# Chunked attention feeding a feed-forward layer on one core: a second buffer for transposed probabilities, moves halved over two queues, and attention groups placed elsewhere

## The chip, the cores and the metric

The kernel runs on one core of one Trainium2 chip. The metric is the device time of one execution in microseconds (us). Five engines work side by side: TensorE (PE, matrix products), VectorE (DVE), ScalarE (ACT), GpSimd (POOL) and SyncE (SP), which here only starts transfers; POOL starts transfers as well.

## The reference

```python
# q, k, v: [8 batches, 8 heads, 576 rows, 64]; chunks of 64 rows attend only to themselves
scores = scale * np.matmul(q_c, k_c.transpose(0, 1, 2, 4, 3))
scores = scores - np.max(scores, axis=-1, keepdims=True)
attn = np.exp(scores)
attn = attn / (np.sum(attn, axis=-1, keepdims=True) + 1e-09)
out = np.matmul(attn, v_c)
# x: [4608 tokens, 512], heads side by side; w_in 512 x 2048, w_out 2048 x 512
h = x @ w_in
g = np.where(h >= 1, h, np.where(h <= -1, 0.0, (h + 1) ** 2 / 4.0))
return (g @ w_out).astype(np.float32)
```

The weights come as float64.

## The kernel before

The 4608 tokens are worked in nine tiles of 512, t = 0 to 8. Tile 0 is the first 512 rows of batch 0 and tile 1 those of batch 1; tile 2 (SINGLE) is the last 64 rows of all batches; tiles 3 to 8 are the batches 2 to 7, taken in pairs (3,4), (5,6), (7,8).

**Weights.** Each of the 16 blocks of w_in (wi) and of w_out (wo) is loaded as 512 KB of words (`load_weight`, L258) and prepared on the chip (`prepare`, L275): ACT and DVE take the float64 words apart and write a high and a low part (parts_wi, parts_wo), with products in three terms afterwards. This is spread over tile 0: before the products of a block of the hidden layer, its weights must be ready.

**Feed-forward part.** For tiles 0 and 1 each of 16 steps j makes a hidden block (`ffn_in`, L560, PE into ps_h), the activation r, its rounding gh and remainder gl (`ffn_split`, L585: ACT L589, DVE L591), and two steps later the products with wo (`ffn_out`, L595) into four sums s = 0 to 3, in the banks ps_o0, ps_o1 and ps_o23, which holds both the third and the fourth. After j = 15 each sum is copied (`store`, L614: even ones by ACT L620, odd ones by DVE L618) into one of four buffers tmp and sent from there to DRAM by SP. Tile 2 (`single`, L936) and the pairs (`whole`, L987) use fewer products, of combined inputs and combined weights. The combined weights are made in tile 1 (`combine_weights`, L791), kept in the DRAM tensor combos, and come back through a ring of six half buffers, which POOL loads (L864). In a pair the second tile's hidden blocks go to DRAM (rest, `put_aside` L982) and come back into r (`fetch` L1017, POOL), and `second_half` (L1023) makes their outputs, during the next stage's products.

**Attention** runs in groups, four to a tile (two heads of a batch's 512 rows each, or the like). For a group: q and k are loaded (SP); `attn_turn` (L393) transposes them by DVE (L400, qT and kT); `scores_of` makes 64 x 64 products on PE into ps_a (L424); `attn_softmax` (L469) takes the maximum (DVE L480), subtracts it (DVE L496), the exponentials (ACT L499), sums (DVE L505), reciprocal (L506, L507) and product e <- e, sm (L512, by POOL for tile 0, else DVE), then a transpose into x (DVE L532) and eight transfers aT <- x (`move`, L518 to L524), of 32 partitions each. Finally `values_of` (L431, PE L446) multiplies aT with v. For tile 1 the subtraction and the sums are made by ACT: eight exponentials of 64 columns that add up as they go (L489). In tile 0 x is not used; PE transposes instead (L391).

The one buffer x is written by DVE and read by the eight moves of the group. Their queue is POOL for the tiles 1, 3 and 4, else SP. aT, v, q and k have two buffers each.

**Where the groups stand.** Tile 0's attention runs at the start; a table SECOND (L1094) puts the scores ("front") and values ("back") of tile 1's groups, and the front of tile 2's first group, at steps j of tile 0. In tile 1 every four steps a `burst` (L1120) takes the values of one group and the scores of the next: groups of tile 2, then the first of tile 3. In tile 2 bursts stand every 13 units of products from the 12th (tiles 3 and 4, with the scores of tile 5's first two groups in the last two), and in the pairs every 15 units.

**What sets the order.** The program does not write instructions engine by engine. Each part goes to a planner (`Plan`, L18 to L129) with an engine, a cost in us, what it reads and writes, and is written out in the order in which it would be ready by those costs; so an edit at one place can move instructions on all engines. Each engine, POOL's and SP's queues among them, works its own list in that order.

## Time and profile before

| | |
|---|---|
| Time, median of 3 runs | 861.07 us (858.66 to 862.81) |
| The profiled execution, its time | 861.77 us |
| Its span | 859.9 us |
| Mean clock granted to TensorE | 0.995 of full |
| PE busy | 830.0 us, 97% of the span |
| DVE busy | 559.2 us, 65% |
| ACT busy | 461.9 us, 54% |
| POOL busy | 276.2 us, 32% |
| Moved by the 16 DMA engines | 162.59 MB, mean 189 GB/s |

The span is the profiled part of the execution; its own time is 1.9 us longer. Idle time is named after what released the engine ("<- DVE h L908": the instruction that wrote h, at line 908). PE's busy time is counted from starts and modelled ends, so that a PE that is busy need not be at its best rate. By the trace's times, tile 0 ends at about 138 us, tile 1 at 228, tile 2 at 335, and the first pair's first half at 475.

### The profile page before, as it was taken

Reading aid. Unit: us, or ns where it says so; the run is one execution under the profiler, and the core shown is the slowest. Engines: PE = TensorE matmul, PEld = TensorE weight load, DVE = VectorE, ACT = ScalarE, POOL = GpSimd, SP = SyncE. Lnnn points to the kernel's source line nnn. Section 1 sums busy time; section 2 is a strip of 40 time slices with the busy share of each in tenths; the row PEclk is TensorE's granted clock in tenths of the full one; section 3 lists DMA queues with packets and bytes.
Section 4 is the critical chain, followed back from the end, with each engine's and each line's share of the span. In section 5 each row is a group of like instructions: output and inputs, shape, how many; then the busy total and the mean of one; then the engine's idle time right before and its main releaser. Section 6 shows DMA issues by size and latency. Waiting matters only on the chain.

```text
span 859.9 us, 16488 instructions
## 1 busy us (share of the span) xinstructions
PE 830.0 (97%) x5918; PEld 682.7 (79%) x5918; DVE 559.2 (65%) x991; ACT 461.9 (54%) x863; POOL 276.2 (32%) x498
## 2 busy tenths in 40 slices
PE   6998999999999997999999999999999999999998
PEld 6776777888887886888888788888887888888786
DVE  4899998999787875676579525665583234344322
ACT  4788884555455554555557324555582245455321
POOL 6235320253456551232232212332232123332210
PEclk9999999999999999999999999999999999999999
DMA  9989973676699996888778617865545254444432
GB/s 235 267 273 253 263 203 81 184 232 207 141 251 247 228 235 174 224 223 225 208 207 217 200 58 208 235 196 176 171 168 184 74 171 166 153 156 151 138 108 73
DMA packets 236368, 162.59 MB, mean 189 GB/s; under 512 B 190464, under 2 KB 203776, under 8 KB 236288
## 3 DMA queue, kind: packets, MB, share of 16 engines
q0 software_dynamic: 33664, 102.79, 36.3%
q1 hardware_dynamic: 201568, 58.50, 29.7%
q8 instruction: 47, 0.77, 0.4%
q10 hardware_dynamic: 1056, 0.26, 0.1%
q14 instruction: 33, 0.27, 0.1%
HBM read 116.39 MB, written 36.70 MB: 178 GB/s over the span
## 4 chain that ended last, share of the span: by engine, by line
PE 65%; issue 11%; DMA 8%; DVE 6%; POOL 6%; SPq 2%; ACT 1%; POOLq 0%; DVEq 0%; ACTq 0%
PE ps_o L604 34%; PE ps_h L885 20%; PE ps_h L570 8%; POOL ring L864 4%; DMA ring<-combos 2%; PE ps_a L446 2%; SPq L333 1%; DMA r<-rest 1%; PE ps_a L424 1%; DMA aT<-x 1%; DMA first_wi<-in_k_dram 1%; POOL rest L984 1%; DMA rest<-r 1%; DVE tmp L296 1%; DVE tmp L301 1%
## 5 line engine op out<-in xcount | busy, mean ns | idle before, releaser
L604 PE MATMUL ps_o<-parts_wo,gh 128*128 128x512 f32 x1152 | 360.5, 394 | 1.9 <-ACT gh L589 1.8
L604 PEld LDWEIGHTS ps_o<-parts_wo,gh 128*128 128x128 f32 x1152 | 212.0, 189 | 46.2 <-ACT gh L589 2.6
L604 PE MATMUL ps_o<-parts_wo,gl 128*128 128x512 f32 x576 | 225.5, 391 | 0.0
L864 POOL DMA_DIRECT2D ring<-combos x224 | 120.5, 539 | 238.7 <-PE ps_h L885 231.0
L591 DVE TENSOR_TENSOR gl<-r,gh 128x512 fp32r<-128x512 f32 x144 | 98.4, 686 | 103.5 <-ACT gh L589 102.9
L589 ACT CAST gh<-r 128x512 fp32r<-128x512 f32 x144 | 88.9, 620 | 137.7 <-PE ps_o L604 78.9
L604 PEld LDWEIGHTS ps_o<-parts_wo,gl 128*128 128x128 f32 x576 | 108.5, 188 | 24.1 <-DVE gl L591 1.4
L908 DVE TENSOR_TENSOR h<-ps_h,snaps 128x512 f32<-128x512 f32 (+1 forms) x96 | 58.9, 614 | 81.3 <-ACT snaps L699 72.9
L918 DVE SCALAR_TENSOR_TENSOR r<-h,r 128x512 f32<-128x512 f32 x88 | 60.2, 684 | 59.3 <-ACT r L917 59.1
L885 PE MATMUL ps_h<-t,ring 128*128 128x512 f32 x360 | 97.2, 389 | 0.0
L699 ACT COPY snaps<-ps_h 128x512 f32<-128x512 f32 (+1 forms) x96 | 50.9, 530 | 84.2 <-PE ps_h L885 83.4
L914 ACT ACTIVATE r<-h 128x512 f32<-128x512 f32 x88 | 55.6, 632 | 68.2 <-DVE h L908 66.5
L570 PE MATMUL ps_h<-xh,parts_wi 128*128 128x512 f32 x256 | 87.1, 398 | 0.8 <-DVE parts_wi L315 0.4
L885 PEld LDWEIGHTS ps_h<-t,ring 128*128 128x128 f32 x360 | 67.6, 188 | 14.0
L885 PE MATMUL ps_h<-xh,ring 128*128 128x512 f32 x192 | 74.9, 390 | 0.0
L917 ACT ACTIVATE r<-r 128x512 f32<-128x512 f32 x112 | 70.6, 630 | 2.6
L885 PE MATMUL ps_h<-b,ring 128*128 128x512 f32 x216 | 60.7, 390 | 0.0
L1020 POOL DMA_DIRECT2D r<-rest x48 | 25.7, 537 | 105.3 <-DVE gl L591 81.4
L885 PE MATMUL ps_h<-set,ring 128*128 128x256 f32 x336 | 50.4, 289 | 8.3 <-DVE h L908 5.5
L885 PEld LDWEIGHTS ps_h<-set,ring 128*128 128x128 f32 x336 | 46.0, 192 | 14.9 <-DVE h L908 6.0
L570 PEld LDWEIGHTS ps_h<-xh,parts_wi 128*128 128x128 f32 x256 | 48.0, 188 | 12.1 <-DVE parts_wi L315 0.9
L524 POOL DMA_DIRECT2D aT<-x x96 | 47.7, 501 | 28.4 <-issue 12.0
(166 smaller groups left out, 1127.3 us busy)
## 6 DMA issues: line engine op xcount, KB each, us to landing
ring<-combos POOLq DMA_DIRECT2D x224, 256.0 KB, 3.8
rest<-r POOLq DMA_DIRECT2D x48, 256.0 KB, 3.3
r<-rest POOLq DMA_DIRECT2D x48, 256.0 KB, 2.9
words_wi<-in_moe_w_in_dram SPq DMA_DIRECT2D x16, 512.0 KB, 7.5
words_wo<-in_moe_w_out_dram SPq DMA_DIRECT2D x16, 512.0 KB, 6.0
v_sb<-in_v_dram SPq DMA_DIRECT2D x128, 64.0 KB, 3.0
out_dram<-tmp SPq DMA_DIRECT2D x32, 256.0 KB, 3.8
combos<-x_parts POOLq DMA_DIRECT2D x32, 256.0 KB, 3.3
```

The costliest lines, as they stand in the source:

```text
L524: queues[queue].dma_start(out=aT[b:b + Q, to], in_=x[a:a + Q, of])
L570: nc.tensor.matmul(out=ps, lhsT=weight["wi", j][:, half, kc * P:(kc + 1) * P], rhs=x, start=(kc == 0 and i == 0), stop=(kc == KC - 1 and i ...
L589: plan.add("act", 0.52, lambda: nc.scalar.copy(out=gh, in_=now(r)), (rkey,), (ghkey,), ahead=ahead)
L591: plan.add("dve", 0.6, lambda: nc.vector.tensor_tensor(out=gl, in0=now(r), in1=gh.bitcast(F32), op=ALU.subtract), (rkey, ghkey), (glkey,), ...
L604: nc.tensor.matmul(out=acc, lhsT=x[:, cols], rhs=weight["wo", j][:, half, :], start=(j == 0 and i == 0), stop=(j == NF - 1 and i == 2),)
L699: "act", cost, lambda: nc.scalar.copy(out=out(), in_=src()), reads, writes, ahead=ahead
L864: plan.add("pool", 0.55, lambda: nc.gpsimd.dma_start(out=ap().bitcast(F32), in_=combos[d][:, n, :].bitcast(F32)), (f"dram{d}_{n}",), (key, ...
L885: nc.tensor.matmul(out=ps[:, :wide], lhsT=w()[:, at:at + P], rhs=y(), start=name in FRESH and i == 0 and k == 0, stop=i == 1 and k == 2, s ...
L908: plan.add("dve", 0.36 if wide == QC else 0.62, lambda: nc.vector.tensor_tensor(out=o(), in0=source[1](), in1=ap(), op=ALU.add), (source[0 ...
L914: plan.add("act", 0.52, lambda: nc.scalar.activation(out=now(r), in_=h(), func=AF.Relu, bias=0.5, scale=0.5), (hkey,), (rkey,), ahead=50)
L917: plan.add("act", 0.52, lambda: nc.scalar.square(out=now(r), in_=now(r)), (), (rkey,), ahead=50)
L918: plan.add("dve", 0.6, lambda: nc.vector.scalar_tensor_tensor(out=now(r), in0=h(), scalar=1.0, in1=now(r), op0=ALU.max, op1=ALU.min), (hke ...
```

## The change

1. **x and its moves.** From the tile 3 on, groups write x and the fourth tmp buffer in turn (x_pair). `move` takes one half: four transfers on SP and four on POOL, with a key each (aT's two halves); for tile 1 both halves stay on POOL.
2. **Stores** of the tiles from 1 on use only the first three tmp buffers.
3. **Sums by ACT** for tile 2's groups as well, as in tile 1.
4. **Places.** The front of tile 2's first group leaves tile 0; three backs (and the fronts beside them) come one step j later, or the last one. In tile 1 a table SPREAD sets the bursts. In tile 2 the last two bursts hold values only. The stage of pair (3,4) has ten bursts from its first unit on, every 13; that of (5,6) eight, every 15; that of (7,8) none.
5. **First loads.** The first three wi and two wo blocks go from SP's queue to POOL's, among the v loads.
6. **Smaller.** A transfer of combined weights to DRAM waits for a later weight to be prepared; the buffers into which `fetch` brings back the second half are taken in another order (r, two aside, r, instead of r, r, two aside).

```diff
+    x_pair = (x_bufs[0], tmp_bufs[3])
...
+    def spare(t):
+        return tmp_bufs[:3] if t > SINGLE - 2 else tmp_bufs
...
-        return emit, (akey, vkey), pkeys
+        return emit, (f"{akey}_0", f"{akey}_1", vkey), pkeys
...
-        sums = t == 1
+        sums = t in (1, SINGLE)
...
-        queue = "pool" if t in (1, SINGLE + 1, SINGLE + 2) else "sp"
...
+        def move(j, queue):
+
+            for i in range(4):
+                a, b = ((2 * j + n) * Q for n in divmod(i, 2))
...
-            xkey, x = x_bufs[turn(t, g) % len(x_bufs)]
+            xkey, x = x_bufs[turn(t, g) % len(x_bufs)] if t <= SINGLE else x_pair[turn(t, g) % 2]
...
-            plan.add(queue, 4.8, move, (xkey,), (akey,), lag=1.7, moving=0.4)
+            for j in range(2):
+                queue = "pool" if t == 1 or j else "sp"
+                plan.add(queue, 2.6, lambda j=j, queue=queue: move(j, queue), (xkey,),
+                         (f"{akey}_{j}",), lag=1.7 if t < SINGLE else 2.5, moving=0.4)
...
-        okey, o = turn_of("tmp", tmp_bufs)
+        okey, o = turn_of("tmp", spare(t))
...
-            plan.add("pool", 0.7, send, reads, (f"dram{d}_{n}",), lag=1.7, moving=0.8)
+            plan.add("pool", 0.7, send, (*reads, f"done_wo{max(2 * p + 1, 5)}"),
+                     (f"dram{d}_{n}",), lag=1.7, moving=0.8)
...
-        return (*r_bufs, aside(0), aside(1))[j % 4]
+        return (r_bufs[0], aside(0), aside(1), r_bufs[1])[j % 4]
...
-        ("q", 0, "sp"), ("k", 0, "act"), ("wi", 0, "sp"), ("q", 1, "sp"), ("k", 1, "sp"),
...
+        ("q", 0, "sp"), ("k", 0, "act"), ("wi", 0, "pool"), ("q", 1, "sp"), ("k", 1, "sp"),
...
-        1: ((front, 0),), 3: ((front, 1),), 5: ((back, 0), (front, 2)), 8: ((back, 1), (front, 3)),
-        11: ((back, 2),), 13: ((back, 3), (front, 4)),
+        1: ((front, 0),), 3: ((front, 1),), 6: ((back, 0), (front, 2)), 9: ((back, 1), (front, 3)),
+        12: ((back, 2),), 14: ((back, 3),),
...
+    SPREAD = {1: (None, 8), 4: (8, 9), 7: (9, 10), 10: (10, 11), 13: (11, 12), 15: (None, 13)}
...
-    run(units, range(12, 12 + 13 * 8, 13))
+    run(units, {12 + 13 * m: (12 + m, 14 + m if m < 6 else None) for m in range(8)})
...
-        run(units, range(8, len(units), 15))
+        n = turn(t, 0) + 2 * NP
+        if t == SINGLE + 1:
+            some = [(None, n), (None, n + 1)] + [(n + m, n + m + 2) for m in range(2 * NP)]
+            run(units, {13 * m: pair for m, pair in enumerate(some)})
+        elif n < ALL:
+            some = [(n + m, n + m + 2 if n + m + 2 < ALL else None) for m in range(2 * NP)]
+            run(units, {8 + 15 * m: pair for m, pair in enumerate(some)})
+        else:
+            run(units, {})
```

POOL's list at the start of the program, before (v_sb and first_wo hold v; e and first_wo the exponentials of tile 0):

```order
L366 DMA v_sb_72<-in_v_dram 64x4x64 x4
L366 DMA v_sb_73<-in_v_dram 64x4x64 x4
L366 DMA first_wo_148<-in_v_dram 64x4x64 x4
L366 DMA first_wo_146<-in_v_dram 64x4x64 x4
L512 TENSOR_TENSOR e_76<-e_76,sm_83 128x512
L837 DMA combos_101<-parts_wi_291 128x4x128 x2
L512 TENSOR_TENSOR e_77<-e_77,sm_84 128x512
L837 DMA combos_104<-parts_wi_380 128x4x128
L512 TENSOR_TENSOR first_wo_148<-first_wo_148,sm_83 128x512
L512 TENSOR_TENSOR first_wo_146<-first_wo_146,sm_84 128x512
```

and after the change (words_wi and words_wo are the weights' words):

```order
L268 DMA words_wi_175<-in_moe_w_in_dram 128x4x256
L268 DMA words_wi_179<-in_moe_w_in_dram 128x4x256
L370 DMA v_sb_72<-in_v_dram 64x4x64 x4
L275 DMA words_wo_200<-in_moe_w_out_dram 128x1024
L370 DMA v_sb_73<-in_v_dram 64x4x64 x4
L268 DMA words_wi_252<-in_moe_w_in_dram 128x4x256
L370 DMA first_wo_148<-in_v_dram 64x4x64 x4
L275 DMA words_wo_307<-in_moe_w_out_dram 128x1024
L370 DMA first_wo_146<-in_v_dram 64x4x64 x4
L516 TENSOR_TENSOR e_76<-e_76,sm_83 128x512
L516 TENSOR_TENSOR e_77<-e_77,sm_84 128x512
L516 TENSOR_TENSOR first_wo_148<-first_wo_148,sm_83 128x512
```

The weights' loads stand among those of v, and the four products of tile 0's softmax behind all of them (the fourth is the row after these); the first transfers of combined weights come later than these.

SP's list towards the end of tile 2, before (aT<-x x8 are the moves of the two groups of tile 5, out_dram the first store):

```order
L347 DMA k_sb_70<-in_k_dram 32x16x32 x4
L366 DMA v_sb_72<-in_v_dram 64x4x64 x4
L347 DMA q_sb_69<-in_q_dram 32x16x32 x4
L347 DMA k_sb_71<-in_k_dram 32x16x32 x4
L524 DMA aT_78<-x_80 32x256 x8
L366 DMA v_sb_73<-in_v_dram 64x4x64 x4
L347 DMA q_sb_68<-in_q_dram 32x16x32 x4
L524 DMA aT_79<-x_80 32x256 x8
L347 DMA k_sb_70<-in_k_dram 32x16x32 x4
L366 DMA v_sb_72<-in_v_dram 64x4x64 x4
L629 DMA out_dram<-tmp_136 64x512 x2
```

and after the change, with tmp_138 the second buffer for x:

```order
L370 DMA v_sb_73<-in_v_dram 64x4x64 x4
L525 DMA aT_78<-x_80 32x256 x4
L351 DMA q_sb_68<-in_q_dram 32x16x32 x4
L351 DMA k_sb_70<-in_k_dram 32x16x32 x4
L525 DMA aT_79<-tmp_138 32x256 x4
L370 DMA v_sb_72<-in_v_dram 64x4x64 x4
L370 DMA v_sb_73<-in_v_dram 64x4x64 x4
L351 DMA q_sb_69<-in_q_dram 32x16x32 x4
L351 DMA k_sb_71<-in_k_dram 32x16x32 x4
L525 DMA aT_78<-x_80 32x256 x4
L633 DMA out_dram<-tmp_136 64x512 x2
```

The moves on SP are four at a time instead of eight, and come from the two buffers in turn; the other four of each group stand on POOL's list.

PE's list where the second half of pair (5,6) starts, right after the last block of the sums before (parts_wo_507, in the change 502, is the first block of the new sums, j = 0, and 627 or 626 the second; ps_o_139 holds the third and the fourth sum), before:

```order
L604 MATMUL ps_o_141<-parts_wo_507,gh_131 128x512 x2
L604 MATMUL ps_o_141<-parts_wo_507,gl_133 128x512
L604 MATMUL ps_o_142<-parts_wo_507,gh_131 128x512 x2
L604 MATMUL ps_o_142<-parts_wo_507,gl_133 128x512
L604 MATMUL ps_o_139<-parts_wo_507,gh_131 128x512 x2
L604 MATMUL ps_o_139<-parts_wo_507,gl_133 128x512
L604 MATMUL ps_o_139<-parts_wo_507,gh_131 128x512 x2
L604 MATMUL ps_o_139<-parts_wo_507,gl_133 128x512
L885 MATMUL ps_h_143<-xh_1_92,ring_2134 128x512
L885 MATMUL ps_h_143<-xl_1_97,ring_2134 128x512
L885 MATMUL ps_h_143<-xh_1_92,ring_2134 128x512
L885 MATMUL ps_h_143<-t_3797,ring_2134 128x512 x3
```

and after the change:

```order
L608 MATMUL ps_o_141<-parts_wo_502,gh_131 128x512 x2
L608 MATMUL ps_o_141<-parts_wo_502,gl_133 128x512
L608 MATMUL ps_o_142<-parts_wo_502,gh_131 128x512 x2
L608 MATMUL ps_o_142<-parts_wo_502,gl_133 128x512
L608 MATMUL ps_o_139<-parts_wo_502,gh_131 128x512 x2
L608 MATMUL ps_o_139<-parts_wo_502,gl_133 128x512
L608 MATMUL ps_o_141<-parts_wo_626,gh_132 128x512 x2
L608 MATMUL ps_o_141<-parts_wo_626,gl_134 128x512
L608 MATMUL ps_o_142<-parts_wo_626,gh_132 128x512 x2
L608 MATMUL ps_o_142<-parts_wo_626,gl_134 128x512
L608 MATMUL ps_o_139<-parts_wo_502,gh_131 128x512 x2
L608 MATMUL ps_o_139<-parts_wo_502,gl_133 128x512
```

The fourth sum's products for j = 0 (the second pair of rows on ps_o_139 with parts_wo_502) have moved behind those of the first two sums for j = 1.

More of the change, by code (lines that the diff above doesn't have):

```diff
@@ L514, in attn_softmax @@
         ), (skey,), (ekey,), port=True)
-        queue = "pool" if t in (1, SINGLE + 1, SINGLE + 2) else "sp"
-        def move():
-            for j in range(2):
-                for i in range(4):
-                    a, b = ((2 * j + n) * Q for n in divmod(i, 2))
-                    to, of = (slice(h * HALF, (h + 1) * HALF) for h in divmod(i, 2))
-                    queues[queue].dma_start(out=aT[b:b + Q, to], in_=x[a:a + Q, of])
+        def move(j, queue):
+            for i in range(4):
+                a, b = ((2 * j + n) * Q for n in divmod(i, 2))
+                to, of = (slice(h * HALF, (h + 1) * HALF) for h in divmod(i, 2))
+                queues[queue].dma_start(out=aT[b:b + Q, to], in_=x[a:a + Q, of])
         if t == 0:
@@ L528, in attn_softmax @@
             plan.add("pe", 0.45, lambda: flip(ps, e), (ekey,), (pkey,), columns=T)
-            plan.add("act", 0.48, lambda: nc.scalar.copy(out=aT, in_=ps), (pkey,), (akey,))
+            plan.add("act", 0.48, lambda: nc.scalar.copy(out=aT, in_=ps), (pkey,), (f"{akey}_0", f"{akey}_1"))
         else:
-            xkey, x = x_bufs[turn(t, g) % len(x_bufs)]
+            xkey, x = x_bufs[turn(t, g) % len(x_bufs)] if t <= SINGLE else x_pair[turn(t, g) % 2]
             plan.add("dve", 0.6, lambda: nc.vector.transpose(
@@ L1118, in hand_over @@
             give("r2", ("r2_0", "r2_1"), F32)
+    SPREAD = {1: (None, 8), 4: (8, 9), 7: (9, 10), 10: (10, 11), 13: (11, 12), 15: (None, 13)}
     def burst(n, m):
-        some = []
-        if n is not None:
-            some.append(values_of(*AT[n]))
-        if m < ALL:
+        some = [values_of(*AT[n])] if n is not None else []
+        if m is not None:
             some.append(scores_of(*AT[m]))
         attn_products(*some, lag=0.8)
-        if m < ALL:
+        if m is not None:
             attn_softmax(*AT[m])
@@ L1130, in burst @@
             attn_split(*AT[n])
-        if m > 3 * NP and m + 1 < ALL:
+        if m is not None and m > 3 * NP and m + 1 < ALL:
             attn_turn(*AT[m + 1])
@@ L1134, in burst @@
             load_heads(*AT[n + 2], "v")
-        if m + 2 < ALL:
+        if m is not None and m + 2 < ALL:
             load_heads(*AT[m + 2], "qk")
@@ L1143 @@
             else:
-                n = 2 * NP + j // 4
-                if j % 4 == 0:
-                    attn_turn(*AT[n + 1])
-                    if j == 0:
-                        load_heads(*AT[n + 2], "qk")
-                if j % 4 == 2:
-                    burst(n, n + 1)
-                if j == NF - 2:
-                    attn_turn(*AT[3 * NP + 1])
-                if j == NF - 1:
-                    burst(None, 3 * NP + 1)
+                if j == 0:
+                    attn_turn(*AT[2 * NP])
+                if j in SPREAD:
+                    n, m = SPREAD[j]
+                    burst(n, m)
+                    if m + 1 < 3 * NP + 2:
+                        attn_turn(*AT[m + 1])
             ffn_in(t, j)
@@ L1172, with run @@
         push(1, j)
-    n = 3 * NP
-    def run(units, at):
-        nonlocal n
-        for k, unit in enumerate(units):
-            if k in at and n < ALL:
-                burst(n, n + 2)
-                n += 1
+    def run(units, bursts):
+        for n, unit in enumerate(units):
+            if n in bursts:
+                burst(*bursts[n])
             unit()
     units = [unit for p in range(NQ) for unit in single(SINGLE, p)]
-    run(units, range(12, 12 + 13 * 8, 13))
+    run(units, {12 + 13 * m: (12 + m, 14 + m if m < 6 else None) for m in range(8)})
     for slot, name in ((0, "t21"), (4, "t31"), (1, "t11"), (5, "b22"), (2, "t41")):
```

6 rows, old and new, of the table first_loads are left out of this document.

## Prediction

> **What bounds the kernel now.** I read the busy time by stage first, to see where TensorE (PE) stands idle and what is full there; then the waits of PE, longest first; then the timeline around the longest. The windows of 20 us hold, after the name of each engine, its busy us, then the clock granted to TensorE, the share of the DMA engines and GB/s:
>
> ```profile
> 0.00:20.00 20.00, 13.29 (x146) 12.12 (x146) 7.74 (x14) 8.37 (x14) 13.49 (x25) 1.00 1.04 225
> 20.00:40.00 20.00, 17.71 (x299) 14.40 (x300) 16.53 (x33) 15.18 (x28) 5.40 (x6) 1.00 0.95 278
> 40.00:60.00 20.00, 19.85 (x127) 16.45 (x126) 19.94 (x39) 17.02 (x50) 6.59 (x12) 1.00 0.87 245
> 60.00:80.00 20.00, 17.16 (x154) 13.38 (x153) 19.12 (x40) 17.29 (x51) 6.58 (x12) 0.91 1.01 283
> 120.00:140.00 20.00, 19.20 (x113) 15.02 (x112) 19.92 (x37) 12.22 (x22) 2.24 (x3) 1.00 0.45 107
> 280.00:300.00 20.00, 19.10 (x230) 16.73 (x229) 17.13 (x33) 10.53 (x22) 11.33 (x23) 1.00 0.92 228
> 320.00:340.00 20.00, 14.46 (x72) 11.88 (x71) 12.48 (x24) 9.44 (x19) 4.14 (x8) 0.91 0.71 181
> ```
>
> PE loses its time in two places. In the first tile VectorE (DVE) works 19 to 20 of each 20 us from 40 on, up to the last weights at about 130, so DVE sets the pace there; before 40 it stands idle for 11.4 us in all (7.9 and 3.5), while the DMA engines are full (1.04 and 0.95). In the third tile, up to 335, the DMA engines are again nearly full (0.92) and PE drops to 14.5 of 20 in the last window. What PE waited for:
>
> ```profile
> PE ps_h L885 <- DVE h L908: 5.5, 1, 5.5
> PE ps_a L446 <- ACT e L489: 4.3, 2, 2.6
> PE ps_h L885 <- DVE x L532: 1.4, 1, 1.4
> PE ps_h L885 <- DMA ring<-combos: 1.3, 2, 0.9
> PE ps_a L446 <- DMA aT<-x: 1.0, 1, 1.0
> ```
>
> The longest wait, 5.5 us, is in the third tile. Its timeline (start, duration, engine, line, and in brackets the idle time before and its releaser):
>
> ```profile
> 317.25 5.25 SPq L347 DMA_DIRECT2D k_sb<-in_k_dram  x4
> 322.61 5.04 SPq L524 DMA_DIRECT2D aT<-x  x8
> 327.74 2.75 SPq L366 DMA_DIRECT2D v_sb<-in_v_dram  x4
> 330.78 0.71 DVE L532 STREAM_TRANSPOSE x<-e 128x512 f32<-128x512 f32 x1 [6.71 <-DMA v_sb<-in_v_dram]
> 332.58 0.41 DVE L908 TENSOR_TENSOR h<-ps_h,snaps 128x256 f32<-128x256 f32 x1
> 333.04 1.65 PE L885 MATMUL ps_h<-set,ring 128*128 128x256 f32 x6 [5.54 <-DVE h L908]
> ```
>
> This is a chain through one buffer. The eight moves aT<-x of the head group before stand on SP's queue behind key loads and are issued from 322.61 to 327.65. Only when they have landed may DVE write x again; it stood 6.71 us for that (the bracket names the v load, which is issued last; the moves hold the buffer). DVE's next products, h at 332.58, come behind it, and PE behind those. The last window's clock, 0.91 over 20 us, is another 1.8 us lost; the same 0.91 stands in 60:80. Every other wait in PE's list is shorter than these.
>
> **Third tile: two x buffers, half moves on two queues.** Now consecutive groups write different buffers, so a move may be late by a whole burst before DVE stands. 5.5 and the clock's 1.8 go: 7.3. What is late next is the rest of that list: x 1.4, ring 1.3, aT 1.0, together 3.7. They come from the same traffic:
>
> ```profile
> 268.51 1.49 POOL L524 DMA_DIRECT2D aT<-x  x3
> 270.43 0.50 POOL L524 DMA_DIRECT2D aT<-x  x1 [0.43 <-DMA ring<-combos]
> 280.76 2.99 POOL L524 DMA_DIRECT2D aT<-x  x6
> L524 POOL DMA_DIRECT2D aT<-x x57 | 28.2, 499 | 14.4 <-DMA ring<-combos 7.2 <-DVE x L532 2.7 <-issue 2.1
> ```
>
> In this tile GpSimd (POOL) issues the moves between its ring loads (28.2 us for 57), and some wait for ring loads to land. With four on each queue POOL has half of that, and two groups' scores leave the tile, but SP takes four more: at 5.04 us for eight, 2.5 us more beside q, k and v. I take 1.9 of the 3.7, half, since halves land no earlier if the DMA engines stay full. Gain 9.2; bounds 3.6 (if full DMA engines add waits as long again as those three, 7.3 - 3.7) and 11.0.
>
> By the Trainium skill (TensorE: Matmul & The Clock Gate, Part 1: The HAM clock gate) the array's clock is halved only after an idle window of about 3.4 us. The trace agrees for the 5.5 us wait, and disagrees in 60:80, where 0.91 follows a wait of 2.59 (quoted next); by the rule the clock term of the first tile would be 0, by the row 1.8.
>
> **First tile without the third tile's group, weights on POOL's queue.** The rows of one group's work on DVE (mean ns before the last bar), and its exps on ScalarE (ACT):
>
> ```profile
> L400 DVE STREAM_TRANSPOSE qT<-q_sb 128x512 f32<-128x512 f32 x32 | 22.4, 701 | 0.0
> L480 DVE TENSOR_REDUCE mx<-ps_a 128x8 f32<-128x512 f32 x34 | 23.2, 684 | 2.6 <-PE ps_a L424 2.4 <-ACT xo L699 0.3
> L496 DVE TENSOR_TENSOR e<-ps_a,mx 128x512 f32<-128x512 f32 x29 | 19.8, 681 | 1.8 <-ACT tb L699 0.8 <-ACT ta L699 0.5 <-ACT xe L699 0.5
> L505 DVE TENSOR_REDUCE sm<-e 128x8 f32<-128x512 f32 x30 | 19.9, 664 | 5.9 <-ACT e L499 5.9
> L512 DVE TENSOR_TENSOR e<-e,sm 128x512 f32<-128x512 f32 x32 | 21.9, 684 | 0.1
> L532 DVE STREAM_TRANSPOSE x<-e 128x512 f32<-128x512 f32 x32 | 22.6, 707 | 11.6 <-DMA v_sb<-in_v_dram 6.7 <-DMA aT<-x 4.1 <-DVE gl L591 0.4
> L489 ACT ACTIVATE e<-ps_a,mx 128x64 f32<-128x64 f32 x32 | 9.5, 328 | 0.1
> L489 ACT ACTIVATION_READ_ACCUMULATOR e<-ps_a,mx 128x1 f32 x32 | 7.1, 221 | 0.0
> 76.82 1.34 PE L446 MATMUL ps_a<-aT,v_sb 64*64 64x64 f32 x32 [2.59 <-ACT e L489]
> ```
>
> Two transposes, maximum, subtraction, sum, product and x: 2 x 0.70 + 0.68 + 0.68 + 0.66 + 0.68 + 0.71 = 4.8 us leave the DVE-bound stretch. They go to the second tile, where sums by ACT save the subtraction and the sum of its four groups (0.68 + 0.66 each, 5.4 in all), so DVE has no more work there than now; ACT has 8 x (0.33 + 0.22) = 4.4 us by durations instead of one exp, but has slack in that tile (12.2 of 20 at 120:140), so that costs nothing; if that cover were gone, a wait like the 2.59 above, four times.
>
> The waits for exps (4.3 us by PE's list, the longer one the 2.59 above) need values that stand too close behind the next group's scores; in the new order one such place (the second back of the first tile) has as little work between as now, the other has more. DVE's pace hides most of that anyway: a term of PE there counts only where DVE is not later.
>
> The start:
>
> ```profile
> 16.33 3.46 SPq L333 DMA_DIRECT2D first_wi<-in_k_dram  x2
> 31.22 0.48 PE L570 MATMUL ps_h<-xh,parts_wi 128*128 128x512 f32 x1
> 32.63 1.04 POOL L512 TENSOR_TENSOR first_wo<-first_wo,sm 128x512 f32<-128x512 f32 x1 [2.20 <-DVE sm L507]
> ```
>
> The last key load now ends its issue at 19.8, behind three weight loads on SP; the last product by POOL runs at 32.63, and the first FFN product on PE at 31.22. With the weights on POOL, q and k stand alone on SP, and each queue gets its share of full DMA engines, so keys may come some 5 us earlier; but the same bytes must land before DVE can prepare weights, and all four products on POOL now stand behind all its 21 loads. DVE could fill at most its 11.4 us idle; I take 1.2 of it (near the lower end, 0, since the same bytes pass through engines at 1.04 and 0.95). Gain 4.8 + 1.2 = 6.0; bounds 1.6 (the longer exps wait stays, 2.6, with its clock, 1.8, and is not covered: 6.0 - 4.4) and 9.0 (DVE 4.8 and 4.2 of its idle time).
>
> **From the second tile to the third.** Stores have three buffers now, and the first x of the alternate buffer comes where the fourth of tmp is also used by the combination of weights: a DVE row must wait for half moves to land, with gl, x parts and store copies behind it. Nothing in the trace shows it; bounds 0 (the products behind it wait for PE anyway) and 2.5 (four moves by SP, half of 5.04). I take 0.8.
>
> **Stores in the pairs.** The fourth copy of a tile must wait until the first's transfer has landed; PE then waits to write that bank. Where the second tile of a pair starts:
>
> ```profile
> 646.12 0.58 ACT L620 COPY tmp<-ps_o 128x512 f32<-128x512 f32 x1
> 646.51 0.62 PE L604 MATMUL ps_o<-parts_wo,gh 128*128 128x512 f32 x2
> 646.73 3.02 SPq L625 DMA_DIRECT2D out_dram<-tmp  x4
> 647.19 0.62 PE L604 MATMUL ps_o<-parts_wo,gh 128*128 128x512 f32 x2
> out_dram<-tmp SPq DMA_DIRECT2D x4, 256.0 KB, 5.6
> 814.30 0.73 PE L604 MATMUL ps_o<-parts_wo,gh 128*128 128x512 f32 x2 [1.50 <-ACT gh L589]
> ```
>
> Three products take 0.68 (646.51 to 647.19). The new order puts 24 products between the end of the first sum and the next write of the last, so PE comes at 646.1 + 8 x 0.68 = 651.5. The copy is free at 646.73 + 5.6 + 0.69 for the copy = 653.0: a wait of 1.5. The like at 812 is about 1.4, but there PE already waits 1.50 for gh; it takes the place of that. At the first pair there is work for 32 products, no wait or 0.5. Net +1.0; bounds 0 and 5.6 (one full landing, more than all three waits).
>
> **Third pair's scores in the first pair's stage.** The stage from 335 to 475 has ten bursts instead of eight, and POOL now carries half moves between ring loads there too. PE loses nothing there now. Bounds -0.3 (SP relieved) and +16 (second rival); I take +0.5, near the rows of the third tile (ring 1.3 in all, under fuller DMA).
>
> **The sum.** The profiled execution's own time is 861.8 (0.7 above the median). 861.8 - 9.2 - 6.0 + 0.8 + 1.0 + 0.5 = 848.9, so 849.0 us. What a measurement of this kernel can tell from no change is about 0.5%, 4.3 us: 856.8 to 865.4 counts as the same.
>
> **Rivals.** First, the transfers and not the queues are the limit: at 1.04 and 0.95 in the first 40 us and 0.92 in 280:300 a load moved to another queue lands no earlier. For it: those rows. Against it: the 5.5 us chain hangs on one buffer, whatever the rate. Then the start gives 0, the first tile keeps the longer exps wait and its clock, half of them covered by DVE's pace (4.8 - 4.4 / 2 = 2.6), and the third tile gives the 7.3 alone: 861.8 - 7.3 - 2.6 + 2.3 = 854.2. This is also what the Trainium skill says (DMA: Bandwidth & Descriptors, Issuing engines are not separate DMA queues): starting transfers from several engines saves only the time to issue them.
>
> Second, slower: half moves delay the ring. In 18 bursts of the pairs' stages POOL issues four moves between ring loads. In the third tile ring waits were 1.3 us in all with eight moves a burst; if the whole products' ring, with no slack left, waited 1.3 in every burst, that is 18 x 1.3 = 23.4, and 849 - 0.5 + 23.4 = 872. It decides from 12.9 / 18 = 0.7 us per burst. Against it: the waits listed for PE name the ring for 1.3 us in all, so the ring has slack outside the third tile now, where POOL stands for the same loads without moves.
>
> Third, better: both exps waits and their clock go (4.3 + 1.8 = 6.1 by PE, if DVE has room) and DVE fills 4.2 of its idle start: first tile 9 or a little more, third tile 11.0, stores 0: 861.8 - 9.0 - 11.0 + 0.8 + 0.5 = 843.
>
> **How the numbers follow.** Forecast 0.53, first rival 0.20, third 0.13, second 0.08, and 0.06 for a sum of small waits that ends within 0.5%. The forecast's own range is 844 to 854; the range reaches to 841 below and to 858 above, for the first rival with 2 to 4 us of store waits. Faster 0.84 (0.53 + 0.20 + 0.13 less 0.02 of the first rival's upper end), same 0.08, slower 0.08.
>
> **What would show it.** Right: PE's wait for h of 5.5 is gone and DVE never stands over 2 us before x; no 0.91 near 320:340; the last weights of the first tile are ready at about 124 instead of 130; the second tile's first product comes 5 to 7 us earlier; waits of 1 to 2 us at ps_o, for ACT or DVE copies, at the pairs' middles. The first rival shows in an unmoved 31.2 and unmoved last weights; the second in waits for ring spread over 335 to 640. The forecast is wrong if PE's loss between 335 and 800 exceeds 5 us, or if the first tile ends less than 2 us earlier.

## The result and the profile after

The changed kernel takes 869.3 us (median of 10 runs, 866.5 to 874.2) where the kernel before takes 862.6 (10 runs beside it, 856.4 to 867.1): a ratio of 1.0095, 95% interval 1.0067 to 1.0123. It is slower by 6.7 us by the medians and by 8 by the ratio, where 12 us faster was forecast, and lies outside the range of 841 to 858. Each trace is of one execution (run 1's took 873.0 us, the longest of its six), and run 10's ratio leaves out one execution of 1661.8 us. The profiled execution took 867.3 us, its span is 865.5 and its mean clock 0.984 (before: 861.8, 859.9 and 0.995).

When each stage starts, by the first product of its kind in the trace, and how long it lasts (us):

| | before: start | length | changed: start | length | difference of lengths | forecast |
|---|---|---|---|---|---|---|
| start, until the first feed-forward product | 0 | 31.2 | 0 | 36.9 | +5.7 | with the next row |
| tile 0 | 31.2 | 103.8 | 36.9 | 99.0 | -4.8 | -6.0 in both |
| tile 1 | 135.0 | 93.2 | 135.9 | 94.0 | +0.8 | +0.8 with its end |
| tile 2 | 228.2 | 107.6 | 229.9 | 107.7 | +0.1 | -9.2 |
| pair (3,4), first tile | 335.8 | 133.1 | 337.6 | 134.0 | +0.9 | +0.5 |
| its second tile and (5,6) | 468.9 | 173.5 | 471.6 | 177.2 | +3.7 | +1.0 with the next row |
| the rest, to PE's last product | 642.4 | 213.3 | 648.8 | 211.8 | -1.5 | |

These add up to 4.9 of the 5.6 us by which the span grew. Tile 2 is as long as before although its wait of 5.5 us is gone, and tile 0 ends no earlier (135.9 against 135.0) although a whole group's work on DVE has left it. What PE waited for in the changed kernel (us in all, times, longest; a wait of 1.2 for kT and one of 0.3 are left out):

```profile
PE ps_a L450 <- DMA aT<-x: 5.2, 2, 3.5
PE ps_o L395 <- DMA first_wi<-in_k_dram: 4.7, 2, 3.3
PE ps_o L608 <- DVE tmp L622: 4.0, 2, 2.5
PE ps_o L395 <- DMA q_sb<-in_q_dram: 3.6, 2, 2.3
PE ps_a L450 <- DMA combos<-parts_wi: 2.4, 1, 2.4
PE ps_o L395 <- DMA k_sb<-in_k_dram: 1.7, 1, 1.7
PE ps_a L450 <- DMA aT<-tmp: 1.6, 1, 1.6
PE ps_h L890 <- DMA ring<-combos: 1.4, 1, 1.4
PE ps_h L1218 <- POOL ident masks.py:199: 1.4, 1, 1.4
```

The wait for h of 5.5 is gone, as forecast. In its place stand waits for moves (aT from x and from the second buffer, 5.2 + 1.6) and store copies (4.0). The two waits for exponentials, 4.3 in all, are now one of 2.4 that is named after combined weights (combos). The values that waited read only aT and v; at the same product (80 to 87 us) other kernels of the new order name the exponentials, so this is most likely the longer of the two. Windows that lost much, beside 80:100, which is shown in the last section (busy us of PE, PEld, DVE, ACT, POOL with instructions in brackets, then clock, DMA share, GB/s):

```profile
0.00:20.00 20.00, 12.14 (x116) 10.90 (x116) 7.01 (x12) 8.07 (x13) 13.32 (x26) 0.83 1.01 236
20.00:40.00 20.00, 16.48 (x236) 14.41 (x237) 12.45 (x27) 12.65 (x23) 5.16 (x6) 0.83 0.90 225
280.00:300.00 20.00, 18.44 (x226) 16.57 (x224) 17.48 (x34) 10.84 (x23) 7.71 (x15) 0.95 0.94 230
300.00:320.00 20.00, 16.50 (x113) 14.17 (x112) 9.63 (x18) 7.03 (x14) 7.96 (x16) 0.88 0.83 193
480.00:500.00 20.00, 17.46 (x150) 13.82 (x142) 16.73 (x31) 7.08 (x12) 4.70 (x9) 0.91 0.82 205
```

DVE is busy 7.01 + 12.45 us of the first 40, before 7.74 + 16.53: it stands idle 4.8 us longer. The clock is 0.95 and 0.88 in 280:320 (20 x 0.05 + 20 x 0.12 = 3.4 us), where before it was lowered once, for 1.8; it is 0.91 after 480 and 0.83 in the first 40 us, where it was 1.00.

**Tile 2.** The timeline of one group, from DVE's transpose on:

```profile
299.22 0.71 DVE L533 STREAM_TRANSPOSE x<-e 128x512 f32<-128x512 f32 x1
300.21 1.99 POOL L525 DMA_DIRECT2D aT<-x  x4
304.64 3.69 SPq L370 DMA_DIRECT2D v_sb<-in_v_dram  x4
308.42 2.47 SPq L525 DMA_DIRECT2D aT<-x  x4
314.55 1.03 PE L450 MATMUL ps_a<-aT,v_sb 64*64 64x64 f32 x32 [3.50 <-DMA aT<-x]
```

x is written at 299.9. POOL starts its half at 300.2. SP's half comes at 308.4, behind q, k and v loads, and lands after 314; the values wait 3.50 us for it. Half of a move is started 8 us late, and the values need both halves. The stage's own account closes: before 5.5 + 1.4 + 1.3 + 1.0 of waits and 1.8 of clock, 11.0; now 5.2 + 1.6 + 1.4 and 3.4, 11.6.

**Stores.** Where the first half of pair (3,4) ends:

```profile
478.77 1.54 SPq L629 DMA_DIRECT2D out_dram<-tmp  x3
483.72 0.69 DVE L622 COPY tmp<-ps_o 128x512 f32<-128x512 f32 x1 [2.17 <-DMA out_dram<-tmp]
484.47 0.73 PE L608 MATMUL ps_o<-parts_wo,gh 128*128 128x512 f32 x2 [2.54 <-DVE tmp L622]
```

The fourth copy (DVE, line 622) waits until the first store, issued at 478.77, has landed; PE stands 2.54 us for the bank.

**Start.** PE's longest wait there, 3.35 us until 26.64, is for the last key load. This is what transfers took from issue to landing in the first 26 us before:

```profile
k_sb<-in_k_dram SPq DMA_DIRECT2D x2, 128.0 KB, 7.2
first_wi<-in_k_dram SPq DMA_DIRECT2D x4, 128.0 KB, 7.9
```

and in the first 28 us of the changed kernel:

```profile
k_sb<-in_k_dram SPq DMA_DIRECT2D x2, 128.0 KB, 10.6
first_wi<-in_k_dram SPq DMA_DIRECT2D x4, 128.0 KB, 9.4
```

Keys land 10.6 and 9.4 us after their issue instead of 7.2 and 7.9. Taking the weights off SP's queue hardly let SP issue the keys earlier: the last pair starts at 15.52 instead of 16.33, the pair before at 10.09 instead of 9.96, because each issue took longer. With the weights' bytes now beside them, they land later. PE's waits before the first feed-forward product are 11.4 us (4.7 + 3.6 + 1.7 in the list above, and 1.4 for the identity matrix), before 8.9. Its work there takes longer too. The filling products, which only keep PE busy between loads, before and in the changed kernel:

```profile
L1213 PE MATMUL ps_h<-ident 128*128 128x128 f32 x56 | 9.1, 321 | 1.4 <-POOL ident masks.py:199 1.4
```

```profile
L1218 PE MATMUL ps_h<-ident 128*128 128x128 f32 x56 | 11.2, 373 | 1.4 <-POOL ident masks.py:199 1.4
```

At the clock of 0.83 of the first 40 us (before: 1.00) one of the 56 took 373 ns instead of 321. So 2.5 of the 5.7 us are waits and the rest is longer busy time (25.5 us against 22.4 up to that product), 2.1 of it in the filling products. The clock of 20:40 is 0.83 to 0.91 in all five kernels that load these weights on POOL's queue and 1.00 in all nine that load them on SP's; in 0:20 it is 0.74 to 0.84 in the five, and 0.91 in three of the nine.

### The profile page after: what moved, and what is told of

It is laid out like the page before. It is cut to its first block, busy times and chain, and to the rows that moved or that the text cites. A ratio compares the mean times of both kernels' runs of the same rounds, so it can differ in the third digit from the quotient of the medians.

```text
span 865.5 us, 16563 instructions
## 1 busy us (share of the span) xinstructions
PE 833.0 (96%) x5890; PEld 687.5 (79%) x5890; DVE 555.3 (64%) x987; ACT 468.7 (54%) x923; POOL 304.8 (35%) x551
## 4 chain that ended last, share of the span: by engine, by line
PE 81%; DMA 8%; DVE 5%; SPq 3%; issue 1%; POOL 1%; ACT 0%; DVEq 0%; POOLq 0%; ACTq 0%
PE ps_o L608 39%; PE ps_h L890 28%; PE ps_h L574 8%; PE ps_a L450 2%; SPq L337 2%; PE ps_a L428 2%; DMA out_dram<-tmp 1%; DMA first_wi<-in_k_dram 1%; DMA k_sb<-in_k_dram 1%; DMA aT<-x 1%; DMA words_wo<-in_moe_w_out_dram 1%; DMA combos<-parts_wi 1%; DMA q_sb<-in_q_dram 1%; SPq L525 1%; POOL combos L841 1%
```

## The experiments

Theory A is that each loss comes from what the change put on a queue or took from a buffer; B, that the DMA engines are full, whatever the queue; C, that the new places of the groups cost the time. In all diffs "-" is the kernel named and "..." stands for lines left out.

| run | us (median) | ratio to before, 95% interval |
|---|---|---|
| the change | 869.3 | 1.0095 (1.0067 to 1.0123) |
| 1 change, loads on SP | 869.2 | 1.0096 (1.0062 to 1.0130) |
| 2 change, moves of tiles 3, 4 on POOL | 863.6 | 1.0020 (0.9998 to 1.0042) |
| 3 change, one x, four store buffers | 860.2 | 1.0001 (0.9970 to 1.0032) |
| 4 change, these three undone | 855.2 | 0.9930 (0.9888 to 0.9972) |
| 5 before, loads on POOL | 863.6 | 1.0031 (0.9996 to 1.0067) |
| 6 before, three store buffers | 865.7 | 1.0048 (1.0018 to 1.0079) |
| 7 before, half moves on two queues | 859.8 | 0.9979 (0.9947 to 1.0011) |
| 8 as 4, tile 2's moves on POOL too | 848.4 | 0.9851 (0.9793 to 0.9908) |
| 9 change, SP's halves on ACT's queue | 876.2 | 1.0174 (1.0133 to 1.0215) |
| 10 before, tile 5's moves on POOL | 855.4 | 0.9927 (0.9901 to 0.9954) |
| 11 as 8, front of tile 2 back in tile 0 | 848.4 | 0.9863 (0.9827 to 0.9900) |
| 12 as 8, two x and three store buffers | 857.7 | 0.9969 (0.9941 to 0.9997) |

**1. The first loads back on SP.**

```diff
-        ("q", 0, "sp"), ("k", 0, "act"), ("wi", 0, "pool"), ("q", 1, "sp"), ("k", 1, "sp"),
+        ("q", 0, "sp"), ("k", 0, "act"), ("wi", 0, "sp"), ("q", 1, "sp"), ("k", 1, "sp"),
...
```

> The change with the list of first loads of before (weights on SP's queue again), all else as changed. Theory A (each loss is made by what the change put on a queue or took from a buffer): the weights on POOL's queue made the keys and the attention of the first tile late, so the first product of the feed-forward part comes back from 36.9 to about 31 us, VectorE's idle time before 40 us falls from 20.5 to about 16, and the first tile ends 4 to 5 us earlier than in the changed kernel: about 865 where the changed kernel has 869. Theory B (the transfers, not the queues, are full in the first 40 us): first product at 36 or 37, time within 1 us of the changed kernel. Theory C (the new places of the attention groups cost the time): the same as B.

The first feed-forward product came at 29.8 and tile 1 began at 131.3 instead of 135.9, as A said; the total did not move (869.2, where A had about 865). PE's waits:

```profile
PE ps_a L450 <- DMA aT<-x: 13.2, 3, 5.8
195.47 1.25 PE L450 MATMUL ps_a<-aT,v_sb 64*64 64x64 f32 x29 [5.84 <-DMA aT<-x]
```

The waits for moves grew from 5.2 to 13.2 us, one of 5.84 in tile 1 among them; there SP's half was started 2.0 us behind POOL's (188.4 against 186.4), after loads of q and k. So tile 1 begins 4.6 us earlier without these loads, and waits for half moves took it back. This trace is of an execution of 873.0 us; at the median of 869.2 the waits may be shorter. The step from "tile 0 ends earlier" to "the kernel ends earlier" failed.

**2. Moves of tiles 3 and 4 on POOL alone.**

```diff
-                queue = "pool" if t == 1 or j else "sp"
+                queue = "pool" if t in (1, SINGLE + 1, SINGLE + 2) or j else "sp"
```

> The change with both halves of the moves on POOL's queue for the groups of tiles 3 and 4 (as all eight were before); the two x buffers stay. Theory A: SP, which now starts 16 transfers a burst in tile 2's stage, is what makes half moves late, so PE's waits for aT (6.8 us in all in the changed kernel) and the lowered clock there (3.4 us) go, and ring waits of 1 to 2 us come: 5 to 9 us faster than the changed kernel, about 862. Theory B (the DMA engines are full there, 0.95): the waits move to the ring or stay, within 2 us of the changed kernel.

0.7% faster than the change, as A expected. No wait for aT is left in the list; those for store copies stayed (4.9 us), and waits for the ring came:

```profile
PE ps_h L890 <- DMA ring<-combos: 4.2, 5, 1.4
300.00:320.00 20.00, 20.00 (x207) 17.25 (x197) 14.37 (x27) 10.21 (x20) 13.28 (x27) 1.00 1.03 227
```

The clock in 300:320 is 1.00 again. Tile 2's stage takes 104.9 us instead of 107.7. This is A, with part of B: 2.8 of the gain came there, and the ring took 2.8 (4.2 - 1.4) of what the moves gave back.

**3. One x buffer and four store buffers.**

```diff
-    x_pair = (x_bufs[0], tmp_bufs[3])
+    x_pair = (x_bufs[0], x_bufs[0])
...
-        return tmp_bufs[:3] if t > SINGLE - 2 else tmp_bufs
+        return tmp_bufs
```

> The change with one x buffer for all groups and the four store buffers of before. Theory A: the waits for store buffers (4.0 us, with a lowered clock of 1.8 at 480:500) go; what the second x buffer saved is at most small here, since the moves are halves: 3 to 5 us faster than the changed kernel, about 865. The rival, that the second x buffer is worth its 5.5 us: VectorE's wait for x comes back with 4 to 6 us in tile 2's stage, and the time is that of the changed kernel or up to 2 us more.

0.9% faster than the change, more than expected. The waits for store copies are gone, the clock after 480 is 1.00, and with one buffer DVE waits 3.6 us in all to write x, where it was 0.4 with two (all groups; idle before it in the last column):

```profile
L533 DVE STREAM_TRANSPOSE x<-e 128x512 f32<-128x512 f32 x32 | 22.6, 707 | 3.6 <-DMA ring<-combos 3.2
480.00:500.00 20.00, 20.00 (x90) 16.53 (x90) 8.04 (x13) 5.55 (x10) 4.30 (x8) 1.00 0.44 136
```

Tile 2's stage takes 104.4 us instead of 107.7, with a wait of 3.7 named after a v load and one of 2.1 for aT left in it. The rival, that the second x buffer is worth its 5.5 us, falls. The run changes the x buffers and the store buffers together, so it gives no price for either alone.

**4. All three undone.** The diffs of 1, 2 and 3 together.

> The three above together: first loads on SP, moves of tiles 3 and 4 on POOL, one x buffer with four store buffers; what stays of the change are the places of the groups, the sums by ScalarE and the order of the r buffers. Theory A: the gains add, about 4.5 + 6 + 3: 855, faster than before by about 0.8%. Theory C: the places cost the time, so it stays above before, 864 to 869.

855.2, where 855 was expected; C falls. That the number was met is partly luck: it was added up from 4.5, 6 and 3, and the parts alone gave 0.2, 5.8 and 9.1. One long wait for moves is left, in tile 1, where tile 2's groups still split their moves over SP and POOL:

```profile
PE ps_a L450 <- DMA aT<-x: 3.4, 1, 3.4
```

**5, 6 and 7. One part alone, put into the kernel before.** The loads:

```diff
-        ("q", 0, "sp"), ("k", 0, "act"), ("wi", 0, "sp"), ("q", 1, "sp"), ("k", 1, "sp"),
+        ("q", 0, "sp"), ("k", 0, "act"), ("wi", 0, "pool"), ("q", 1, "sp"), ("k", 1, "sp"),
...
```

> The kernel before with only the list of first loads of the change (five weights on POOL's queue). If the loads are what made the start late: first product of the feed-forward part at 36 to 37 us instead of 31.2, VectorE's idle time before 40 us up by 4 to 5, the first tile's end and the whole 4 to 5 us later, about 866. The rival (the end of the first tile is set by VectorE's sum of work, and waits later on swallow or add the difference, as in the run with the loads back on SP, whose total did not move): first product late, but the total within 2 us of before.

The first product came at 35.9 and tile 1 began at 139.3 instead of 135.0, 4.3 late; the profiled span grew by 3.3. The total, 863.6 against 863.1, is not told from before, as the rival had it and not the 866 expected. The stores:

```diff
-        okey, o = turn_of("tmp", tmp_bufs)
+        okey, o = turn_of("tmp", tmp_bufs[:3] if t > SINGLE - 2 else tmp_bufs)
```

> The kernel before with only three of the four store buffers for the tiles from the second on. If the store buffers cost what the changed kernel shows at 481 and 657 us: waits of PE at ps_o for a copy of 1.5 to 2.5 us each at two or three of the pairs' middles, with a lowered clock after one of them, 3 to 6 us slower than before, about 866. The rival: the wait needs SP's queue full of half moves as well, so alone it costs under 2 us.

0.5% slower, 2.6 us by the medians, a little less than the 3 to 6 expected. PE's waits at ps_o:

```profile
PE ps_o L604 <- ACT gh L589: 3.8, 2, 2.2
PE ps_o L604 <- DVE tmp L618: 1.1, 1, 1.1
```

The copies alone cost 1.1; gh, 1.8 before, now 3.8. The halves:

```diff
...
-        queue = "pool" if t in (1, SINGLE + 1, SINGLE + 2) else "sp"
...
-            plan.add(queue, 4.8, move, (xkey,), (akey,), lag=1.7, moving=0.4)
+            for j in range(2):
+                queue = "pool" if t == 1 or j else "sp"
+                plan.add(queue, 2.6, lambda j=j, queue=queue: move(j, queue), (xkey,),
+                         (f"{akey}_{j}",), lag=1.7 if t < SINGLE else 2.5, moving=0.4)
```

> The kernel before with only the moves cut in halves over SP and POOL; one x buffer, four store buffers, groups where they were. If SP's queue makes half moves late: in tile 2's stage PE waits for aT by 3 us or more in all, the ring waits of 1.3 us go, and VectorE's wait for x, which needs the later of the two halves now, stays or grows to several us: 861 to 867. The rival (the split helps, as fewer transfers stand between ring loads): 857 to 860.

My expectation for the time was wrong: it is the same as before, 859.8, in the rival's range. Its waits and windows tell why:

```profile
PE ps_a L446 <- DMA aT<-x: 7.4, 2, 4.4
260.00:280.00 20.00, 17.04 (x209) 15.14 (x209) 14.09 (x27) 8.99 (x19) 7.99 (x16) 0.91 0.92 208
300.00:320.00 20.00, 15.60 (x143) 13.83 (x142) 12.85 (x26) 7.65 (x16) 7.44 (x15) 0.91 0.84 191
```

The waits for aT came (7.4, and 0.91 twice, 3.6 us), as A said. But the wait of 5.5 for h went as well, with one x buffer. In this stage the split trades one for the other, and the stage lasts 106.7 us, before 107.6.

**8. Tile 2's moves on POOL too.**

```diff
-                queue = "pool" if t in (1, SINGLE + 1, SINGLE + 2) or j else "sp"
+                queue = "pool" if t <= SINGLE + 2 or j else "sp"
```

> The kernel with three parts undone, and in addition both halves of the moves of tile 2's groups (issued in tile 1) on POOL. If SP's half is late there too: the wait of 3.4 us for aT at 189 us, with what it costs of the clock, goes: 3 to 5 us faster than with three undone, about 851. The rival: POOL, which then stands between the combined weights' transfers and eight moves, makes the same wait, total unchanged at 855.

848.4 us, 1.5% faster than before and, with run 11, the fastest of all; 6.8 faster than run 4, where 3 to 5 was expected. No wait for aT is left; behind the start the longest are these:

```profile
PE ps_a L450 <- ACT e L493: 2.5, 1, 2.5
PE ps_h L890 <- DMA ring<-combos: 1.1, 1, 1.1
```

Tile 0 ends at 130.0, 5.0 earlier than before; 1.8 of that is an earlier first feed-forward product (29.4 against 31.2; it varies from 29.4 to 31.2 among the nine kernels with these loads on SP). Tile 2 takes 98.4 us, 9.2 less.

**9. SP's halves on ACT's queue.**

```diff
-                queue = "pool" if t == 1 or j else "sp"
+                queue = "pool" if t == 1 or j else "act"
```

> The change with the SP halves of the moves started by ScalarE's queue instead. If SP's serial issue (16 transfers a burst) is what makes the halves late, PE's waits for aT in tile 2's stage (6.8 us in the changed kernel) go to under 2 us, and the lowered clock of 280:320 with them: 4 to 8 us faster than the changed kernel, 861 to 865. If the DMA engines are the limit (0.94 busy there), the waits for aT, the ring or q and k stay at 5 us or more in sum, and the time within 2 us of the changed kernel. ScalarE itself has 9 us of 20 to spare there, but exps that stand behind its transfers may add 1 us.

Both expectations for the time missed. The waits for aT are gone to the last, and tile 2's stage takes 102.1 us instead of 107.7: SP's list it was, not the DMA engines. But each half holds ACT itself, in its order, and 37.4 us of ACT's idle time, in twelve places, is named after these transfers:

```profile
173.65 2.44 ACTq L525 DMA_DIRECT2D aT<-x  x4
PE ps_o L608 <- DVE tmp L622: 9.4, 2, 7.1
PE ps_h L574 <- DVE r L585: 3.7, 1, 3.7
```

Tile 1 took 101.2 us instead of 94.0 and the stage from 471.8 on 184.2 instead of 177.2, with one wait of 7.1 us for a store copy and the clock at 0.74 after 480. The buffer came free late: ACT's copies there stand behind such a half and a rounding that waited for its r (480.05; in the changed kernel 477.24), and the transfer that empties the buffer left SP at 487.51 only, behind loads of v, q and k. The edit moved these places too, so how much of the loss is ACT's holding is not shown.

**10. Tile 5's moves on POOL, in the kernel before.**

```diff
-        queue = "pool" if t in (1, SINGLE + 1, SINGLE + 2) else "sp"
+        queue = "pool" if t in (1, SINGLE + 1, SINGLE + 2, SINGLE + 3) else "sp"
```

> The kernel before with only the queue of tile 5's moves turned from SP to POOL (all eight, one x buffer). If the 5.5 us wait at 327 us comes from the moves' place behind key loads on SP's queue, it goes with one buffer too, with its lowered clock: 4 to 7 us faster than before, about 856. If it comes from having one buffer, VectorE still waits for the moves of the group before and the wait stays at 3 us or more: 861 to 863.

0.7% faster than before by one term in one line, as expected, and with one x buffer. The wait for h is gone:

```profile
PE ps_h L885 <- DMA ring<-combos: 5.0, 4, 2.5
L532 DVE STREAM_TRANSPOSE x<-e 128x512 f32<-128x512 f32 x32 | 22.6, 706 | 5.0 <-DMA aT<-x 2.4 <-DMA ring<-combos 2.1
320.00:340.00 20.00, 19.82 (x106) 16.39 (x104) 16.15 (x30) 12.31 (x24) 8.73 (x17) 1.00 1.02 254
```

DVE stands idle before x for 5.0 us in all, where it was 11.6, the ring takes 5.0 of PE's time (1.3 before), and the clock of 320:340 is 1.00. DVE's order around the wait is the one of before; the moves are issued from 318.3 to 323.5 instead of 322.6 to 327.7. The 5.5 us wait came from the moves' place on SP's list.

**11. The front of tile 2's first group back in tile 0.**

```diff
-        12: ((back, 2),), 14: ((back, 3),),
+        12: ((back, 2),), 14: ((back, 3), (front, 4)),
...
-    SPREAD = {1: (None, 8), 4: (8, 9), 7: (9, 10), 10: (10, 11), 13: (11, 12), 15: (None, 13)}
+    SPREAD = {4: (8, 9), 7: (9, 10), 10: (10, 11), 13: (11, 12), 15: (None, 13)}
...
-                    attn_turn(*AT[2 * NP])
+                    attn_turn(*AT[2 * NP + 1])
+                    load_heads(*AT[2 * NP + 2], "qk")
```

> The fastest kernel so far (three parts undone, tile 2's moves on POOL) with the first group of tile 2 turned back into the first tile (its transposes, scores and softmax). If VectorE's sum of work sets the end of the first tile, that end comes 4 to 5 us later (134 to 135 instead of 130.0), 0.9 of it given back in the second tile by the scores that leave it: about 852, 3 to 4 us slower. The rival (the tile's end is set by the exps wait and the weights' arrival): less than 2 us slower.

Nothing was lost: 848.4. Tile 1 begins at 131.9 instead of 130.0, and the difference is gone at the end, as the rival had it. But the place in the new order is one step later than in the kernel before, and that decides what the run can tell. Before, the group's two transposes, maximum and subtraction on DVE stood ahead of the last weights; here all of its work stands behind them, and they are 1.0 us later only (125.3 against 124.3). The first lines are of before, the others of this run:

```profile
122.48 0.70 DVE L400 STREAM_TRANSPOSE qT<-q_sb 128x512 f32<-128x512 f32 x1
129.14 0.68 DVE L315 TENSOR_TENSOR parts_wi<-tmp,parts_wi 128x512 fp32r<-128x512 f32 x1
```

```profile
125.34 0.68 DVE L319 TENSOR_TENSOR parts_wi<-tmp,parts_wi 128x512 fp32r<-128x512 f32 x1
126.54 0.70 DVE L404 STREAM_TRANSPOSE qT<-q_sb 128x512 f32<-128x512 f32 x1
```

So the run does not bring back the old order, and does not test whether DVE's work ahead of the weights sets the pace.

**12. The buffers of the change in the fastest kernel.** The diff of 3, turned round, on 8.

> The fastest kernel (first loads on SP, moves up to tile 4 on POOL, places as changed), but with the second x buffer and the three store buffers of the change put back. If the store buffers are the largest term that stayed: PE waits for store copies at the middles of the first two pairs by 1.5 to 3 us each, with a lowered clock after the first, and the second x buffer gives nothing back: 4 to 8 us slower than 848.4, so 852 to 856. The rival (the second x buffer is worth as much as the stores cost): 847 to 850.

857.7, so 9.4 us slower than 8, a little more than expected:

```profile
PE ps_o L608 <- DVE tmp L622: 7.6, 3, 3.6
240.00:260.00 20.00, 15.68 (x142) 13.01 (x140) 13.04 (x27) 8.74 (x18) 10.49 (x20) 0.91 0.90 261
460.00:480.00 20.00, 17.74 (x189) 13.93 (x187) 17.90 (x34) 10.09 (x17) 6.29 (x12) 0.92 0.97 248
```

Three waits for store copies, 7.6 us in all with the longest, 3.6, at the passage from tile 1 to tile 2, and the lowered clock after two of them (1.8 + 1.6): 11.0, as much as the difference of the spans (855.9 - 844.9). It does not close so well: run 8 lost 1.8 of clock in 80:100 after a wait of 2.45, and run 12 nothing there after one of 2.59 at the same product, so 9.2 of the 11.0 are named. The second x buffer is part of the edit, and its own part is not told apart.

## Why the prediction was wrong

**Tile 2, -9.2, measured +0.1: the step that failed most.** Right was that the 5.5 us wait and its clock would go. Wrong was why, and what comes next. The prediction read the wait as a matter of one buffer; run 10 removed it with one buffer by the moves' queue, run 7 with one buffer by the halves, and in run 3 the stage was 3.3 us shorter with one buffer than with two. And the prediction put all that was late next at 3.7 us and took half of it. It saw that "SP takes four more: at 5.04 us for eight, 2.5 us more beside q, k and v", and did not ask who waits for the later half: the values need both, and SP's half stands behind a group's loads (308.4 against 300.2). With 6.8 us of aT waits and 3.4 of lowered clock the stage was where it had been, below the bound of 3.6 given for it, which had left the clock out. The first rival, the DMA engines, was wrong here in the main: the same bytes on POOL (2) or on ACT (9) end these waits, though in run 2 the ring waited 2.8 us longer.

**Start and tile 0, -6.0, measured +0.9.** The DVE idle time was misread: 7.9 us in the first 20 came from the weight-load column beside DVE's; DVE was busy 7.74 there, so its idle time before 40 was 15.7, not 11.4. More, the sign was wrong. The prediction had 1.2 of this idle time filled; it grew by 4.8 with the weights on POOL's queue, as much as was counted as saved by the group that left. The keys landed later after their issue, and PE worked at a lower clock. The first rival had the start as zero; tile 1 began 4.3 to 4.6 later by it (runs 1, 5), but in neither run did the total move by that. Whether the 4.8 of DVE work is a real term stays open. For it: in run 8, with the loads back on SP, the last weights come at 124.3 instead of 129.1, as foretold, and in the changed kernel at 129.9, with DVE 4.8 longer idle before 40. Against its size: only two transposes, maximum and subtraction (2.7 us) stood ahead of the last weights before. The later backs, with one exps wait (2.5) in the place of two (4.3), may have their part in the tile's gain in run 8; no run separates them. As foretold, one exps wait stayed.

**From tile 1 to tile 2, +0.8.** In the changed kernel tile 1 with this passage is 0.8 longer, but not by the wait foretold, which did not show there; PE's work for the scores that the tile took over is the likely cause. That the number agrees is luck. In run 12 PE did wait at this passage, 3.6 us, above the bound of 2.5; but DVE's copy there waited for a store to land (3.47 us, until 249.57), not for half moves.

**Stores, +1.0, measured +3.7 and -1.5.** The mechanism is the one foretold, and at the middle of (5,6) the wait is 1.47 for the 1.5 worked out. At (3,4), "no wait or 0.5" was 2.54 with 1.8 of clock: the transfers stood behind a half move on SP (475.45 to 478.67), and this is most of the +3.7. At (7,8), neither the old nor the new wait came. The last row has the 1.47 more and the old 1.50 less; why it is 1.5 shorter is not known. Run 12 prices the three store buffers together with the second x buffer at 9.4 us with their clock, above the bound of 5.6, which again had no clock in it.

**Pairs, +0.5.** Measured +0.9; PE is busy all through this stage in both kernels, so this is its work, likely the two groups' scores. The second rival, ring waits in every burst, did not come: PE's list has the ring once, 1.4 us, at 251 in tile 2.

Of the signs named beforehand, "wait for h gone" and "DVE never over 2 us before x" came true in a kernel that was slower, so they tested the chain and not the time; the signs of being wrong (tile 0 less than 2 us earlier, over 5 us lost between 335 and 800: 2.5 + 1.5 + 1.8) came true as well. The kernel ended on the slower side by none of the rivals. Each was one mechanism alone; what happened is that POOL's queue took back in the start, SP's in tile 2 and the store buffers in the pairs what other parts had gained. The forecast's 849 is what run 8 reaches, with three parts of the change undone and a fourth turned.

**Queues and DMA engines.** "Issuing engines are not separate DMA queues" (the Trainium skill, DMA: Bandwidth & Descriptors) says that starting transfers from several engines saves only the time to issue them. The start agrees (keys 10.6 us to landing instead of 7.2 with other loads beside them). In tile 2 that time of issue was the bound: SP's list ran 8 us late, and another queue ended the wait.

## What to carry to other kernels

A transfer cut over two queues is as late as the fuller queue: before splitting, list what stands on each queue at that place and when the consumer needs the last piece. A buffer that is lent from a pool of stores must be priced where that pool turns round, with the time to landing and with the clock that a PE wait of 2 us mostly takes along (it fell at 31 of the 35 waits of 2 us or more that the 14 kernels show after 40 us). A wait at a buffer may be cured by the reader's place in its queue (run 10, one line) as well as by another buffer.

## What the runs showed of the hardware

The granted clock fell after short waits of PE: 0.91 in 480:500 of the changed kernel with one wait of 2.54 us, and 0.91 and 0.92 in run 12 after 3.56 and 2.26, some 1.7 us lost each time. The Trainium skill (TensorE: Matmul & The Clock Gate, Part 1: The HAM clock gate) gives an idle window of about 3.4 us for this; here shorter ones did it, down to one of 1.56 at 296.6 in the changed kernel (the 0.95 of 280:300). In windows of 1 us each lowered stretch after 40 us, up to PE's last product, adds up to 1.7 us lost, or to two or three times that; before, 334:336 shows 0.50. The length of the wait alone does not decide: the changed kernel lost 1.7 after a wait of 2.35 us at 86, and run 12 nothing after one of 2.59 at 82 at the same product (the window of each, with columns as above, and the product that waited):

```profile
80.00:100.00 20.00, 16.51 (x122) 13.11 (x121) 19.96 (x40) 17.50 (x44) 8.60 (x15) 0.91 0.91 291
86.00 1.10 PE L450 MATMUL ps_a<-aT,v_sb 64*64 64x64 f32 x32 [2.35 <-DMA combos<-parts_wi]
```

```profile
80.00:100.00 20.00, 17.46 (x130) 13.59 (x131) 19.97 (x39) 17.06 (x40) 8.81 (x14) 1.00 1.04 315
81.70 0.90 PE L450 MATMUL ps_a<-aT,v_sb 64*64 64x64 f32 x32 [2.59 <-DMA combos<-parts_wi]
```

What tells them apart was not tried. And four transfers of 32 KB held ScalarE's list for 2.44 us (run 9, at 173.65), in which it computed nothing.
